# Warm-up dummies tied to one bank, one weight block loaded earlier, half-wise turning back and a classical second pair, with a new plan of the whole order, in an attention and feed-forward kernel

## The chip, the cores and the metric

The kernel runs on one core of a Trainium2 chip. The metric is device time in microseconds (us), from several runs of the same program; lower is better. Beside the times there is one profiled execution, whose trace lists every instruction of each engine: TensorE (PE for matmuls, PEld for its weight loads), VectorE (DVE), ScalarE (ACT), GpSimd (POOL) and SyncE (SP), and every transfer (DMA).

## What is computed

Attention over 4 batches, 8 heads, 768 tokens and head size 64, in which a token sees the 4 first tokens ("sinks") and the 128 last ones up to itself; then a feed-forward part over all 3072 tokens of 512 values, with 2048 hidden values and a squared relu:

```python
def _attn_ref(q, k, v, n_sink, window):
    scores = scale * np.matmul(q, k.transpose(0, 1, 3, 2))
    keep = is_sink | in_window          # pos < 4, or 0 <= rel < 128
    scores = np.where(keep, scores, -1000000000.0)
    a = np.exp(scores - np.max(scores, axis=-1, keepdims=True))
    return np.matmul(a / (np.sum(a, axis=-1, keepdims=True) + 1e-09), v)

def _moe_ref(x, w_in, w_out):
    r = np.maximum(x @ w_in, 0.0)
    return (r * r) @ w_out
```

Inputs and output are float32; the kernel's matmuls take bfloat16.

## The kernel before

**Work of a batch.** A batch has 6 token tiles of 128 tokens, taken as three pairs: tokens 0 to 255 (pair 0), 256 to 511 (pair 1), 512 to 767 (pair 2). q and k are brought into head-by-token form (`qkT`): in batches 0 and 1 by TensorE transposes into a PSUM tile `pt` (line 642) with a copy out of it (line 336 or 334), in batches 2 and 3 by transposing transfers that SP issues (line 596). For tokens 0 to 511 of batch 0, q and k come as float32 (`qr`, line 491) and are first cast to bfloat16 (`qs`); everything else is cast while it is loaded, by transfers from POOL's queue (`qn`, `v`, `w_in_sb`, `w_out_sb`). Then come the scores (`ps`, line 749; in pair 0 of batch 0 with a bias matmul, line 742), exp on ACT (`expm`, line 769), the window's mask (line 781 on DVE, or two selects on POOL, line 360), the scores of the sinks (`pk`, line 708), the values (`po`, line 817), a division by the sum (lines 833, 834), and the turning back of tokens into columns (`bridge`, `px`, line 866, copied to `xT`; in batches 2 and 3 a transposing transfer, line 848). Heads go in pairs; `m` is one of four such pairs.

**Feed-forward.** `layer1` (line 883) makes a block of 1024 hidden results a token tile's width at a time into a PSUM tile `pm` (line 894), 16 matmuls of 256 columns or 8 of 512; relu (line 905 on ACT, 907 on DVE) frees the bank, and a square (lines 914, 916) makes `gT`. There are four loads of `w_in`, each for four of the sixteen hidden blocks. The second product is taken for a pair of token tiles. `layer2` (line 920) is the classical form: 32 matmuls of 512 columns (line 935) in eight parts, and one copy out for each tile. `layer2_fast` (line 980) is a Strassen-Winograd form: four sums on DVE (line 1004), seven products of 8 matmuls of 256 columns (line 1046, named c, d, a, b, c, d, a), and sums of quarters on DVE and ACT (lines 1055 to 1116). It also needs four differences of `w_out`, made once on DVE (`weight_sums`, line 963). In batch 0, pair 0 is classical (line 1187) and all other pairs are fast.

**PSUM.** Two pools of two tiles, `att` and `den`, each tile two banks. `layer1` and the second product use `den`; attention uses `att`, and in batches 0 and 1 partly both.

**What sets the order.** The order on each engine isn't written out. `Plan.run` (line 185) is a list scheduler that runs while the kernel is built: each operation has a key (a due time), estimated costs by engine, its predecessors and the PSUM or SBUF slots that it takes. `PLACES` and `NUDGES` (lines 22 and 54) are tables of numbers that shift and stretch keys by group and by operation; `LATENCY` (line 17) and the transfer estimates (lines 19, 20, 471) enter the starts. So a change of any of these can move every instruction. Only the transfers are chained by hand, in the order in which lines 1133 to 1153 call the loads.

**Dummies.** `warm(dst)` (line 324) puts matmuls of the identity ahead of a block while the plan's time is below 34 us, as many as half of the planned gap holds at 0.056 us, at most 40. They write into the first half of the tile that the block will use, or into its half `h`. `touch` (line 341) declares which accesses to a tile lie in different banks, so that they don't wait for each other; dummies aren't told to it.

**The loads from POOL's queue** at the start: v of tokens 0 to 255, v of tokens 256 to 511, the four `w_in` blocks, q and k of tiles 4 and 5, v of these, the four `w_out` blocks, then batch 1.

**The turning back** (lines 858 to 880) is made in two halves of heads, each with its own copy; both wait for all norms (divisions) of the pair of tiles.

Of the kernel before, what the change touches and what calls it, by code (L numbers as in the profile page):

```python
# [12 lines left out]
BF16 = mybir.dt.bfloat16  # L13
# [3 lines left out]
LATENCY = 0.186  # L17
# [5 lines left out]
    ('att', 0, 0): (0.21, 1.17, -0.18), ('att', 0, 1): (-0.08, 1.08, 0.04), ('att', 0, 2): (0.015, 1.83, -0.6),  # L23
    ('att', 1, 0): (-0.085, 1.44, -0.04), ('att', 1, 1): (-3.34, 2.24, -0.4), ('att', 2, 0): (0.295, 1.46, 0),
    ('att', 2, 1): (-0.735, 0.82, -0.14), ('att', 2, 2): (0.025, 0.88, -0.04), ('att', 3, 0): (0.825, 0.51, 0.08),
    ('att', 3, 1): (0.095, 1.16, -0.02), ('att', 3, 2): (0.325, 0.67, 0.48), ('ev', 0, 1): (0.215, 0.47, 0.16),
    ('ev', 0, 2): (1.935, 1.29, -0), ('ev', 1, 0): (-0.22, 1.16, 0.06), ('ev', 1, 1): (-0.285, 0.65, 0.86),
    ('ev', 1, 2): (0.14, 0.86, -0.46), ('ev', 2, 0): (1.38, 1.32, 0.66), ('ev', 2, 1): (-0.32, 0.82, -0.4),
    ('ev', 2, 2): (0.3, 1.21, 0.76), ('ev', 3, 1): (-0.895, 0.85, -0.64), ('ev', 3, 2): (-0.26, 1, -0.38),
    ('l1', 0, 0): (-0.02, 0.85, 0), ('l1', 0, 1): (0.405, 1, 0.24), ('l1', 0, 2): (0, 0.79, -0.02),  # L30
    ('l1', 1, 0): (0.3, 1.96, 0.08), ('l1', 1, 2): (3.445, 0.3, 0.28), ('l1', 2, 0): (-0.385, 0.71, -0.22),
    ('l1', 2, 2): (-1.92, 1.74, 0.24), ('l1', 3, 0): (0.42, 1.87, 1.06), ('l1', 3, 2): (-0.165, 0.51, 0.16),
    ('l2', 0, 0): (0, 0.95, 0.08), ('l2', 0, 1): (0.22, 1.1, -0.04), ('l2', 0, 2): (-1, 1.11, 0.42),
    ('l2', 1, 0): (2.155, 0.65, 0.4), ('l2', 1, 1): (0.61, 0.79, -0.26), ('l2', 1, 2): (0.4, 1.99, -0.22),
    ('l2', 2, 0): (0.875, 0.26, -2.14), ('l2', 2, 1): (-0.115, 0.6, -0.08), ('l2', 2, 2): (-0.295, 0.98, -0.44),
    ('l2', 3, 0): (-0.02, 1.05, 0.2), ('l2', 3, 2): (-0.69, 0.96, 0.5), ('prep', 0, 0): (0.005, 1.06, -0.62),
    ('prep', 0, 1): (0.635, 0.51, -0.2), ('prep', 1, 0): (0.015, 1, 0), ('prep', 1, 1): (0.055, 1.01, -0.02),
    ('prep', 2, 0): (0.195, 1.11, 0.1), ('prep', 3, 0): (0, 0.84, 0), ('sink', 0, 0): (0.105, 0.86, -0.2),
    ('sink', 0, 1): (-0.105, 0.96, 0), ('sink', 1, 0): (0.93, 1.41, 0.22), ('sink', 1, 1): (-0.025, 1.08, -0.76),
    ('sink', 2, 0): (0.025, 0.99, -0.24), ('sink', 3, 0): (0.215, 1, 0), ('sum', 0, 1): (0, 1.16, -0.08),  # L40
    ('sum', 1, 0): (0.18, 0.44, -2.08), ('sum', 1, 1): (-2.945, 1.06, 1.12), ('sum', 1, 2): (-0.45, 2.49, -1.34),
    ('sum', 2, 0): (0.665, 0.25, 0.82), ('sum', 2, 1): (0, 2.44, 1.56), ('sum', 2, 2): (-0.28, 1.76, 0.08),
    ('sum', 3, 0): (-0.17, 1.59, 0.46), ('sum', 3, 1): (-0.725, 0.7, -0.46), ('sum', 3, 2): (0.055, 0.7, 0.36),
    ('turn', 0, 0): (-0.175, 0.89, 0.1), ('turn', 0, 1): (0.18, 0.58, -0.68), ('turn', 0, 2): (-0.03, 1.45, -0.2),
    ('turn', 1, 0): (-0.195, 1.03, 0.18), ('turn', 1, 1): (-0.035, 0.63, 0.46),
    ('turn', 1, 2): (-0.585, 1.98, -2.12), ('turn', 2, 0): (0.015, 0.99, 0.38),
    ('turn', 2, 1): (-0.365, 1.36, -0.38), ('turn', 2, 2): (0, 0.98, 0.32), ('turn', 3, 0): (-0.1, 1.14, -0.28),
    ('turn', 3, 1): (-0.16, 1.26, -0.72), ('turn', 3, 2): (0.025, 0.92, -0.1), ('val', 0, 0): (-1.295, 0.62, -0.4),
    ('val', 0, 1): (0, 0.95, 0.16), ('val', 0, 2): (0.155, 1.03, -0.5), ('val', 1, 0): (0.015, 0.93, 0),
    ('val', 1, 1): (-0.145, 0.98, 0), ('val', 1, 2): (0.04, 1.25, 0.08), ('val', 2, 0): (-1.09, 0.51, -1.08),  # L50
    ('val', 2, 1): (-0.015, 0.93, -0.28), ('val', 2, 2): (-0.235, 0.96, -0.24), ('val', 3, 0): (-0.245, 0.84, 0.08),
    ('val', 3, 1): (0.755, 2.5, -0.58), ('val', 3, 2): (1.78, 2.4, 0.76), ('wt', 0): (-0.14, 1.32, -0.32),
}
NUDGES = {
    4: (-0.25, 0.48), 16: (-0.103, -0.3), 17: (0.038, -0.06), 18: (0.083, 0.08), 19: (0.017, -0.28),
    20: (0.005, -0.12), 21: (-0.026, -0.38), 23: (-0.015, 0.38), 24: (0.111, 0.4), 25: (-0.017, -0.2),
    26: (0.014, -2.46), 27: (0.063, -0.74), 28: (-0.07, -0.12), 29: (-0.064, 0.02), 30: (-0.047, -0.76),
    31: (-0.001, -0.04), 32: (0.102, 1.86), 33: (0.261, 0.22), 34: (-0.211, -0.62), 35: (0.056, 0.08),
    36: (0.061, -0.32), 37: (-0.006, 0.32), 38: (-0.013, -0.16), 40: (-0.269, -1.14), 41: (0, 0.04),
    42: (0.024, 0.16), 43: (-0.059, -0.22), 44: (0, -0.66), 45: (-0.003, 0), 46: (0.043, 0.26), 47: (0.059, -0.02),  # L60
    48: (0.013, 0.18), 49: (0.124, 0.08), 50: (0.004, -0.26), 51: (-0.136, 0.02), 52: (-0.049, 0.1),
    53: (-0.159, -1.08), 54: (0, 0.02), 56: (0.067, -0.6), 57: (0, 0.02), 60: (-0.263, 0.58), 61: (-0.153, -0.44),
    62: (-0.003, 0.66), 64: (-0.003, 0), 65: (0.037, 0), 66: (-0.097, 0), 67: (-0.046, 0.46), 68: (-0.002, -0.06),
    69: (0.035, 0.36), 70: (-0.001, -0), 72: (0.291, -0.52), 73: (0, -0.08), 74: (-0.036, 0.94), 75: (0.15, 0.32),
    76: (0.011, 0), 77: (0.008, 0.96), 78: (-0.024, 0.12), 80: (-0.015, 0.76), 81: (-0.139, 0.24), 82: (-0.002, 0),
    83: (0.01, 0.02), 84: (0.213, -0.06), 85: (0, -0.08), 86: (0.063, -0), 87: (-0.175, -0.2), 88: (0.107, 0.16),
    89: (0, 0.08), 90: (-0.001, 0.1), 91: (-0.657, 0.04), 93: (-0.008, 0.14), 94: (0.003, 0.1), 95: (0, -0.14),
    96: (-0.002, -0.34), 97: (0.019, -0.18), 98: (0.406, 0.84), 99: (0.027, 0.06), 100: (0.113, 1.1),
    101: (-0.031, 0), 102: (0.23, 0.96), 104: (0.103, 0), 105: (0.005, 0), 106: (-0.073, -0.4), 107: (0.108, -0.4),
    109: (-0.009, 0), 110: (0.403, 0.66), 111: (0.405, 0.56), 112: (0.003, -0.34), 113: (-0.056, 0.2),  # L70
    116: (-0.199, 0.7), 118: (0.001, 0.02), 119: (0.108, 0.72), 120: (0.101, 0.18), 121: (0, -0.22),
    122: (-0.22, -0.52), 124: (-0.004, 0.04), 125: (0.004, 0), 126: (0.03, 0.52), 127: (0.116, -0.3),
    129: (0.001, 0.1), 130: (0.006, -0.14), 131: (0.119, -0), 132: (-0.003, 0.04), 134: (-0.008, 0),
    135: (-0.352, 0.32), 136: (-0.299, 0.48), 138: (-0.093, -0.06), 139: (0.157, -0.2), 140: (0.067, 0.5),
    141: (0.005, 0), 142: (-0.106, -0.4), 143: (-0.12, 0.46), 144: (0.004, 0), 145: (-0.15, -0.48),
    146: (-0.007, -0.26), 147: (0, 0.2), 148: (0, -0.14), 149: (0.177, 0.66), 150: (-0.355, -1.88),
    151: (0.001, 0.14), 152: (-0.098, 0), 153: (-0.035, 1.38), 155: (0.012, 0), 156: (0, 0.08),
    157: (-0.089, -0.02), 159: (0.057, -1), 160: (0.168, -1.88), 161: (-0.004, -0.18), 162: (0.047, -0.08),
    163: (0, -0.6), 164: (-0.073, 0.08), 165: (-0.032, 0), 166: (-0.004, 0), 167: (-0.302, -0.06),
    168: (0.377, 0.62), 169: (0, -0.14), 170: (-0.277, -0.92), 171: (-0.012, -0.38), 172: (0.119, 0.86),  # L80
    173: (0.031, 0.56), 174: (-0.06, -0.52), 176: (0, -0.38), 177: (0.051, -0.42), 178: (-0.009, 0),
    180: (-0.375, -0.08), 181: (-0.432, 1.04), 183: (0.386, -0.12), 184: (-0.014, 1.16), 185: (-0.027, -0.08),
    186: (-0.114, 0), 188: (0.093, -0.74), 189: (0.391, 0.06), 191: (-0.01, -1.12), 192: (0.023, 0),
    193: (0.001, -0.58), 194: (0.116, 0.16), 195: (0.016, 0.04), 197: (0.278, -0.1), 198: (-0.228, 0.08),
    199: (-0.593, -0.7), 200: (-0.017, 0), 201: (-0.016, -0.18), 202: (-0.011, 0.16), 205: (0.016, -0.06),
    206: (-0.312, -0.04), 207: (0, -1.04), 208: (0.018, -0.02), 209: (0.069, -0.26), 210: (0.405, -0.24),
    211: (0.007, -0.36), 212: (0.148, 0), 213: (0.195, 0.2), 214: (-0.14, -1.18), 215: (-0.006, 0),
    216: (0.058, -0.6), 217: (0.015, 0.06), 218: (0.121, 0.56), 219: (0.009, -0.28), 220: (-0.112, 0.08),
    221: (0.051, 0.44), 222: (0.078, 0.16), 224: (0, -0.02), 225: (-0.16, -0.96), 226: (-0.589, -1.1),
# [172 lines left out]
def kernel(  # L262
# [11 lines left out]
    nc = tc.nc  # L274
# [954 lines left out]
```

## Time and profile before

| what | us |
|---|---|
| median of 3 runs | 219.59 (219.2 to 219.82) |
| the profiled execution, its own time | 219.53 |
| its span, first to last instruction | 217.5 |
| TensorE matmuls busy | 206.9 (95% of the span) |
| DVE busy | 150.1 (69%) |
| ACT busy | 117.8 (54%) |
| POOL busy | 97.3 (45%) |
| granted TensorE clock, mean | 0.999 |

The profile has several views. The page gives busy time and the span in 40 slices, one digit for tenths of a slice. The view by stage gives the busy time of each engine between two moments. The chain in order of time follows the work that ended last back to what released it; each of its pieces has a start, a length and what it was. The timeline lists instructions in order of time, with a count, and in square brackets how long the engine sat idle before and what released it. A line number such as L894 is that of the kernel before. All times are counted from the first instruction.

### The profile page before, as it was taken

To read this page: it belongs to the slowest core of one execution; us is meant where nothing else is said; L and a number is where in the kernel's file an instruction comes from. 1 tells how busy PE (TensorE), PEld (TensorE's weight loads), DVE (VectorE), ACT (ScalarE), POOL (GpSimd) and SP (SyncE) were. 2 spreads that over 40 slices of the span, in tenths; PEclk is the share of its full clock that TensorE was granted. 3 is DMA by queue.
4 is the path that set the end of the run, shared out by engine and by line. 5 is a ranking of instruction groups with operands and counts; after the bars stand their busy time and mean duration, and the time that the engine had idled before them with its cause. 6 is when DMAs were issued, how large, how long until landed. Compare 5 with 4: busy or idle time off the path is not lost.

```text
span 217.5 us, 5286 instructions
## 1 busy us (share of the span) xinstructions
PE 206.9 (95%) x2222; PEld 163.5 (75%) x2225; DVE 150.1 (69%) x280; ACT 117.8 (54%) x149; POOL 97.3 (45%) x134
## 2 busy tenths in 40 slices
PE   7799899999999999996999999999999999999992
PEld 7558795689878855585988775579887775799892
DVE  5565476698898837599687755667886747476942
ACT  2596557466765668878570744576512353663210
POOL 7997877699998383589453000410340000000000
PEclk9999999999999999999999999999999999999999
DMA  5999999999999999999979962001303113002022
GB/s 188 264 179 205 165 210 205 158 112 203 155 131 149 196 164 174 132 129 126 106 92 151 190 167 103 0 0 27 65 10 142 53 24 121 3 2 96 3 96 96
DMA packets 93351, 26.06 MB, mean 120 GB/s; under 512 B 86800, under 2 KB 91280, under 8 KB 93328
## 3 DMA queue, kind: packets, MB, share of 16 engines
q0 software_dynamic: 69248, 12.59, 79.1%
q1 hardware_dynamic: 23896, 13.07, 27.9%
q8 instruction: 17, 0.28, 0.5%
q10 hardware_dynamic: 184, 0.07, 0.1%
q14 instruction: 6, 0.05, 0.1%
HBM read 27.30 MB, written 6.29 MB: 154 GB/s over the span
## 4 chain that ended last, share of the span: by engine, by line
PE 81%; POOL 5%; DMA 5%; DVE 4%; ACT 2%; issue 1%; POOLq 0%
PE pm L894 33%; PE py L1046 31%; PE po L817 6%; PE ps L749 4%; DMA w_in_sb<-in_moe_w_in_dram 4%; PE py L935 3%; POOL v L521 2%; DVE sg L1004 2%; PE pt L642 2%; DMA qr<-in_k_dram 1%; POOL expm L360 1%; DVE r L907 1%; PE px L866 1%; ACT expm L769 1%; PE ya L1046 1%; POOL vs L690 1%
## 5 line engine op out<-in xcount | busy, mean ns | idle before, releaser
L894 PE MATMUL pm<-xT,w_in_sb 128*128 128x256 bf16 (+1 forms) x576 | 89.2, 308 | 1.8 <-DVE r L907 1.6
L894 PEld LDWEIGHTS <-w_in_sb 128*128 128x128 bf16 x576 | 62.3, 114 | 20.9 <-issue 3.3
L905 ACT ACTIVATE r<-pm 128x1024 bf16<-128x1024 f32 x39 | 40.0, 1025 | 42.4 <-PE pm L894 39.9
L769 ACT ACTIVATE expm<-ps 128x1024 bf16<-128x1024 f32 (+1 forms) x48 | 43.4, 953 | 20.3 <-PE ps L749 20.2
L360 POOL TENSOR_SCALAR_AFFINE_SELECT expm<-expm 128x512 bf16<-128x512 bf16 x34 | 24.8, 756 | 49.9 <-ACT expm L769 47.3
L1046 PEld LDWEIGHTS <-gT 128*128 128x128 bf16 x368 | 34.1, 98 | 4.6 <-issue 0.6
L916 DVE TENSOR_TENSOR gT<-r 128x1024 bf16<-128x1024 bf16 x34 | 24.3, 716 | 16.0 <-ACT r L905 15.6
L1046 PEld LDWEIGHTS <-sg 128*128 128x128 bf16 x264 | 25.0, 98 | 3.8 <-issue 0.3
L1046 PE MATMUL py<-wt,gT 128*128 128x256 bf16 x176 | 22.8, 273 | 0.0
L1046 PE MATMUL py<-wt,sg 128*128 128x256 bf16 x176 | 22.5, 273 | 0.0
L1046 PE MATMUL py<-w_out_sb,gT 128*128 128x256 bf16 x160 | 20.8, 273 | 0.0
L817 PEld LDWEIGHTS <-expm 128*128 128x128 bf16 x352 | 16.6, 97 | 3.7 <-POOL expm L360 1.2
L817 PE MATMUL po<-v,expm 128*128 128x65 bf16 x352 | 18.3, 193 | 1.1 <-POOL expm L360 0.9
L834 DVE TENSOR_TENSOR xn_sb<-po,rc 128x512 bf16<-128x512 f32 (+1 forms) x28 | 17.2, 615 | 1.0
L914 ACT ACTIVATE gT<-r 128x1024 bf16<-128x1024 bf16 x14 | 14.6, 1055 | 0.3
L749 PE MATMUL ps<-qkT 64*128 64x128 bf16 (+1 forms) x256 | 14.6, 238 | 0.0
L781 DVE TENSOR_TENSOR expm<-expm,tri 128x1024 bf16<-128x1024 bf16 x15 | 10.8, 723 | 4.8 <-ACT expm L769 3.1
L749 PEld LDWEIGHTS <-qkT 64*128 64x128 bf16 x256 | 8.0, 94 | 7.5 <-issue 6.4
L833 DVE RECIPROCAL rc<-po 128x8 f32<-128x8 f32 (+1 forms) x28 | 5.5, 197 | 11.7 <-PE po L817 11.6
L817 PE MATMUL po<-vs,es 128*128 128x65 bf16 x128 | 13.0, 193 | 0.0
L907 DVE TENSOR_SCALAR r<-pm 128x1024 bf16<-128x1024 f32 x9 | 11.0, 1220 | 2.3 <-PE pm L894 2.3
L817 PEld LDWEIGHTS <-es 128*128 128x128 bf16 x128 | 11.7, 97 | 0.0
(77 smaller groups left out, 250.9 us busy)
## 6 DMA issues: line engine op xcount, KB each, us to landing
out_dram<-osb SPq DMA_DIRECT2D x11, 512.0 KB, 2.8
v<-in_v_dram POOLq DMA_DIRECT2D x24, 128.0 KB, 5.6
qn<-in_k_dram POOLq DMA_DIRECT2D x20, 128.0 KB, 9.5
qn<-in_q_dram POOLq DMA_DIRECT2D x20, 128.0 KB, 8.0
w_in_sb<-in_moe_w_in_dram POOLq DMA_DIRECT2D x4, 512.0 KB, 10.4
w_out_sb<-in_moe_w_out_dram POOLq DMA_DIRECT2D x4, 512.0 KB, 10.6
qr<-in_k_dram SPq DMA_DIRECT2D x4, 256.0 KB, 5.2
qr<-in_q_dram SPq DMA_DIRECT2D x4, 256.0 KB, 5.0
```

The lines of the kernel that those rows point to most:

```text
L360: nc.gpsimd.affine_select(out=e_tile, in_=e_tile, compare_op=ALU.is_ge, fill=fill, base=i - 1, pattern=[[0, n], [1 if i else -1, 128]], ch ...
L749: nc.tensor.matmul(ps[:, h2, o:o + w], lhsT=qkT_sb[r, m, 1, c, :], rhs=qkT_sb[r, m, 0, qb:qb + w // 128, :], start=(i == 0 and not biased) ...
L769: nc.scalar.activation(out=x[:, :, o:512], in_=bank_t["s", b, s, m][:, :, o:512], func=AF.Exp, scale=scale)
L781: nc.vector.tensor_mul(y, y, tri.rearrange("p (o a) c -> p o (a c)", o=1).to_broadcast([128, 4, 256]))
L817: touch(("po", b, s, m0), e, nc.tensor.matmul(pv[:, i, h2, :], lhsT=lhsT, rhs=rhs, start=(n_ == 0), stop=(n_ == len(mms) - 1)), j)
L834: touch(("po", b, s, m0), e, nc.vector.tensor_tensor(out=xn_sb[:, 2 * s:2 * s + 2, 128 * (m0 + j0):128 * (m0 + j0 + nj)].rearrange("p i (j ...
L894: nc.tensor.matmul(pm[:, i, :], lhsT=w_in_sb[:, fb // 4, kb, fb % 4:512:4], rhs=xT[:, c0 // 256:(c0 + cw) // 256, kb, :], start=(kb == 0), ...
L905: nc.scalar.activation(out=o, in_=h, func=AF.Relu)
L907: nc.vector.tensor_scalar_max(o, h, 0.0)
L914: nc.scalar.activation(out=g, in_=r, func=AF.Square)
L916: nc.vector.tensor_mul(g, r, r)
L1046: ins = nc.tensor.matmul(y_, lhsT=x[:, i, :], rhs=r_, start=(first or tail and n == 2) and i == 0, stop=i == HB - 1, skip_group_check=not ...
```

## The change

- `warm` takes the name of the tile and its half, tells `touch` of each dummy, and makes at most 26 of them instead of 40.
- `w_in` block 0 is loaded behind v of tokens 0 to 255 and ahead of v of tokens 256 to 511.
- Each half of the turning back waits for the norms of its own heads.
- In batch 0, pair 1 is classical too.
- The plan's numbers are new: `LATENCY`, one transfer estimate, one surcharge on a load, and the two tables `PLACES` and `NUDGES` in full. No operation has other arithmetic by this.

```diff
-LATENCY = 0.186
+LATENCY = 0.122
...
-    def warm(dst):
+    def warm(dst, key=None, h=0):
...
         if P.now < WARM_UNTIL:
-            for _ in range(min(40, int(0.5 * P.gap / 0.056))):
-                nc.tensor.matmul(dst, lhsT=ident, rhs=ident, start=True, stop=True,
-                                 is_transpose=dst.dtype == BF16)
+            for _ in range(min(26, int(0.5 * P.gap / 0.056))):
+                ins = nc.tensor.matmul(dst, lhsT=ident, rhs=ident, start=True, stop=True,
+                                       is_transpose=dst.dtype == BF16)
+                if key:
+                    touch(key, "pe", ins, h)
...
-    ROW = {512: 0.03, 1024: 0.046}
+    ROW = {512: 0.03, 1024: 0.052}
...
-(0.7 if (b, m0, ti, g) == (0, 1, 1, 0) else 0.0)
+(0.7 if (b, m0, ti, g) == (0, 0, 0, 0) else 0.0)
...
-                        warm(pt[:, 0, 0:128])
+                        warm(pt[:, 0, 0:128], ("pt", b, m, g))
...
-                            warm(po[:, js[0], 0:128])
+                            warm(po[:, js[0], 0:128], ("po", b, s, m0), js[0])
...
-                        warm(px[:, h, 0:128])
+                        warm(px[:, h, 0:128], ("px", b, s), h)
...
-                    br = op(at(fs + 0.36), {"pe": 0.235}, bridge, after=norms + older_layer1,
+                    br = op(at(fs + 0.36), {"pe": 0.235}, bridge,
+                            after=norms[len(norms) * h // 2:len(norms) * (h + 1) // 2] + older_layer1,
...
     load_v(0, 0, None, [("qk", 0, 3, 0, 0)])
+    load_w_in(0)
     load_v(0, 1)
-    for i in range(4):
-        load_w_in(i, None if i == 0 else None)
+    for i in range(1, 4):
+        load_w_in(i)
...
-            if b == 0 and u < 1:
+            if b == 0 and u < 2:
                 layer2(b, u, lambda i, part, u=u: 0.408 + 0.466 * (4 * part + 2 * u + i) / 24, by_part=True)
```

What the scheduler makes of it, as the built program shows: the first burst has 26 dummies instead of 39, then four transposes, then ten more dummies. POOL's queue begins with two v tiles, `w_in` block 0, the third v tile, a cast of a k tile, the fourth v tile, `w_in` blocks 1 and 2, the triangles, two selects, the masks, and `w_in` block 3; before, it had four v tiles, four `w_in` blocks, four q and k tiles, a v tile, the triangles, the masks and four selects. On TensorE, the third `w_in` block's matmuls come right behind the turning back of pair 1. The first part of batch 0's classical pair 1 comes just ahead of the transposes of batch 1's last two token tiles, the other seven between there and the first layer-1 block of batch 1; the fast pair 2 now comes within that stretch too. In batch 1 the layer-1 blocks of tokens 512 to 767 now come ahead of those of tokens 0 to 511, whose eight relus all stand on ACT. SP's store of pair 1 stands ahead of the last six of batch 2's twelve transposing transfers, behind the store of pair 2.

## Prediction

> **What bounds the kernel now.** First the page's header and slices, then busy time by stage, then the chain in order of time, then the timeline of the first 25 us.
>
> ```profile
> span 217.5 us, 5286 instructions
> ...
> PE   7799899999999999996999999999999999999992
> ```
>
> TensorE is idle only in slices 0 to 1, a little in 2 to 4, in one slice near 100 us, and in the last. I cut the stages there:
>
> ```profile
> 0.00:24.40 24.40, 19.67 (x269) 16.03 (x270) 13.78 (x39) 15.33 (x20) 21.19 (x38) 1.00 1.29 206
> 24.40:56.49 32.09, 31.92 (x347) 26.43 (x347) 24.24 (x42) 19.95 (x25) 26.47 (x34) 1.00 1.81 174
> 56.49:100.40 43.91, 43.91 (x502) 32.13 (x499) 33.61 (x62) 30.73 (x40) 30.88 (x41) 1.00 2.18 154
> 100.40:102.40 2.00, 0.36 (x6) 0.17 (x6) 2.00 (x3) 1.93 (x2) 1.99 (x4) 1.00 1.27 86
> 102.40:213.50 111.10, 111.09 (x1112) 88.70 (x1111) 76.40 (x137) 49.59 (x63) 16.73 (x22) 1.00 0.40 72
> ```
>
> Columns: length, then busy time of PE, PEld, DVE, ACT, POOL. From 24.4 to 213.5 us TensorE runs back to back but for 2 us, while DVE is full in exactly those 2 us. So there are three things to win: the start, the pause at 100, and TensorE work itself. The chain shows what made the first two:
>
> ```profile
> 9.69 7.63 DMA w_in_sb<-in_moe_w_in_dram
> ...
> 17.61 0.88 POOL v L521
> ...
> 18.55 0.56 POOL tri L360 x2
> ...
> 21.14 2.51 POOL expm L360 x4
> ...
> 23.69 0.87 PE po L817 x23
> ...
> 98.89 2.30 DVE sg L1004
> 101.19 1.15 DVE r L907
> ...
> 102.38 1.91 PE pm L894 x16
> ```
>
> At the start POOL waits for a w_in landing before it can issue a v load, and only then builds triangles and masks for which TensorE stands until 23.7. At 100 us the layer-1 block waits for its bank, held by a relu queued on DVE behind four Winograd sums. And the dummies:
>
> ```profile
> 1.50 4.17 PE L329 MATMUL pt<-ident 128*128 128x128 bf16 x39 [1.50 <-POOL ident L384]
> ...
> 6.58 0.38 PE L329 MATMUL pt<-ident 128*128 128x128 bf16 x4 [0.69 <-ACT qkT L334]
> ...
> 10.07 0.38 PE L329 MATMUL pt<-ident 128*128 128x128 bf16 x4 [0.89 <-ACT qkT L334]
> ...
> 15.06 0.27 PE L329 MATMUL po<-ident 128*128 128x128 bf16 x2 [0.41 <-DVE xn_sb L834]
> ```
>
> A dummy waits for the reader of the tile's other half, and the true transposes or values stand behind it.
>
> **Part by part.** *Dummies.* The cap goes from 40 to 26. The first burst is 39 x 107 ns = 4.2 us and ends at 5.5; 26 end at 1.50 + 2.8 = 4.3, while the first cast is ready at 4.1 (3.65 + 0.43): 1.2 us earlier for the first transpose. The waits of 0.69, 0.89 and 0.41 go, since a dummy is now tied to its own bank. What is late next is the load: the last q tile is cast at 10.37, so the later half of the front moves by about 0.6 us at most from this. Against the smaller cap speaks the Trainium skill ("TensorE: Matmul & The Clock Gate", "What's actually happening"): full clock comes only after about 3.4 us of sustained work, and 26 dummies are 2.8. The trace went to 56 ns spacing 3.85 us after its first dummy. By the rule alone, with 26 dummies and then idleness, one more window at half speed doubles about 1 us of real matmuls: +1 us in the front. But four transposes and ten more dummies now follow at once (14 x 107 ns = 1.5), so work is unbroken to about 5.7: I take 0, range 0 to +1, and even +1 lies in slack shown below.
>
> *First weight block earlier.* On POOL's queue its issue (0.77) moves past two v issues (0.88 to 1.1 each). Loads land one after another: v at about one per us from 11.3 to 14.2, then w_in at 17.3 (9.69 + 7.6) and 19.9 (10.44 + 9.4), the last at 25.0. So block 0 lands at about 12.3 + 3 = 15.3, the two passed v tiles at about 17.3 instead of 14.2, and blocks 1 to 3 where they were. The values of tokens 256 to 511 first run at 19.43 now, behind a layer-1 block; in the new order they come at about 18.5, so the v delay is covered by 1 us (without cover: up to 1).
>
> *Turning back in halves.* The first half needs only two norms instead of four. DVE's two copies (0.42 each) then no longer both follow the last norm: about 0.3 us, no instructions added.
>
> *POOL.* In the new order triangles (0.56) and one select stand ahead of w_in block 3, masks too; v tiles 4 and 5 no longer stand ahead of the triangles. POOL takes one cast of a k tile (nearest row: its 128x512 copy, 0.61), ahead of the fourth v issue. Block 3 is then issued at about 18 instead of 11.9, still 4 us ahead of block 2's landing (22.5), so the load stream isn't starved; cost 0, up to +1.
>
> With these, layer 1 starts at about 16.7 instead of 17.68, its second block at 19.9 (its weights), the third at 22.5 (its weights land 11.17 + 11.3) instead of 24.40: the front gains 1.9 us.
>
> *Where that goes.* From there to the transposes of batch 1's last two token tiles the new order has ten layer-1 blocks at 1.75, nine classical parts at 0.87 and about 7.0 us of transposes, scores, sinks and values: 32.3 us, so TensorE arrives at 54.8. (Before, 24.40 to 56.49 held 32.1: one part less, one turning back of 0.45 more, 0.2 of small gaps.) But the last q tile is issued at 49.96 and lands 6.1 us later, at 56.03; the load engines were busy without a break until then, and the bytes ahead of it are the same. So these transposes start at about 56.1 instead of 56.49. Of the 1.9 us, 0.2 pay for more work ahead, 1.3 become a new wait for a load, 0.4 are kept. Behind that wait stand, on TensorE, the second score block of tokens 256 to 511 of batch 1 and the next classical part, and behind them ACT's exps and DVE's sums for the third pair; they have nothing else to do, so the wait costs its own length and no more.
>
> *Classical second pair.* 32 matmuls of 512 columns at 0.215 (four in 0.86 in the chain) = 6.9 against 56 of 256 at 0.109 (eight in 0.87) = 6.1: +0.8 us of TensorE, in full, as it is the bound. 0.87 of it stands ahead of 56.1, where TensorE would wait anyway, so behind that point the work is 0.06 less than before. DVE loses four sums (0.69 each) and about 2 us of quarter sums for one eviction near 0.6. On SP the pair's store now stands ahead of the q transposes of batch 2's tiles 2 and 3: it waits for the eviction near 76.1, where the old store let them go at 77.4 (landing 86.5); scores need them at 88.6 by the same walk. Covered by 2 us.
>
> *The pause at 100.* The fourth sum took 2.38 us where the first took 0.69: it began at 98.81, while POOL issued a load to 99.19 and then ran two selects to 100.43. The skill ("SBUF — State Buffer", "Who interferes with whom") has a DVE operation with two SBUF inputs blocked for the whole of a GpSimd instruction that reads SBUF, by which whoever starts first goes first: the sum would have been done at 99.5. The row shows it behind the load issue too; by the row each such sum is a risk of 1.7 us. In the new order, the layer-1 blocks of batch 1's first 512 tokens come behind those of the last 256, all their relus stand on ACT, and no sums of that pair lie between them. I walked the queues: relus of 1.02 against block pairs of 1.73, plus eight exps; each bank comes free 0.5 to 2 us ahead of use. So I take the pause (2.03) as gone.
>
> *Sum.* Behind 56.49 the old run has 157.0 us to its last matmul; less 2.03 and 0.1 of small waits, less 0.06: 154.8. 56.1 + 154.8 = 210.9, plus the unchanged tail of 4.0 (213.5 to 217.5): span 214.9. The profiled execution took 219.53 for 217.5, 2.03 around it: 216.9. It stands 0.06 below the median of 219.59, which I neglect.
>
> **Rivals.** (1) *The pause comes back*, as ACT or DVE become the bound around 85 to 105 or in the stretch where the classical pair and the next fast pair both hold a "den" bank (55 to 68) and attention has two "att" banks left. For it: ACT has some 15.5 us of relus and exps in 16.5 us there. Against it: the slack above. 1 to 2 us return: 217.9 to 218.9, likeliest 218.5. Chance 0.28.
> (2) *The load isn't the limit* at 56: were q ready by 54.8, all the front's gain is kept, 1.2 less: 215.6. For it: POOL issues the last loads late, and may issue them 0.6 earlier; against: the unbroken load share of slices 1 to 20. Chance 0.12.
> (3) *Slower.* The classical pair holds its bank for 20 us (54.8 to 75.5, in pieces between other work). In that time seven score blocks and transposes need both "att" banks, each freed only after two exps (1.94 a pair) of the block before; the slack I found for three of them is 0.5 us. If ACT slips past it, each block waits for its exps: 7 x 0.6 = 4.2 on top: 221.1. It decides from 2.7 us of such waits on. Nothing in the old run shows it, as there no pair shared the banks for so long. Chance 0.05.
> (4) *The new order changes nothing*: front gain all lost at the load, pause replaced in full: 219.6. Chance 0.03.
> The forecast has 0.52.
>
> **Numbers.** A measurement can tell 0.3% (0.66 us) from no change. Faster than 218.9: forecast 0.52, (2) 0.12, three quarters of (1), 0.21: 0.85. Within: 0.09; slower 0.06. The range reaches from (2) to the upper end of (1): 215.5 to 218.9; the forecast alone with its unknowns (clock 0 to +1, waits of 0 to 0.8) is 216.2 to 217.7.
>
> **What would show it.** Dummies of the first burst end near 4.3 and no dummy waits for ACT or DVE. First layer-1 block near 16.7, third near 22.5. A PE wait of about 1 us released by a qn load near 55 to 56. No gap over 0.5 us from 57 to the end, PE's last matmul near 210.9. I am wrong if the first clock row is later than 6.5, if PE waits for exps or norms between 57 and 75, or for a relu between 85 and 105.

## The result, and the profile after

The changed kernel takes 217.34 us (median; 216.81 to 217.92) against 219.63 for the kernel before in the same comparison: ratio 0.990, 95% interval 0.987 to 0.993, 2.2 us faster. The prediction was 216.9. The changed kernel's profiled execution took 216.81 us, the least of its four, for a span of 215.1. A few executions of some kernels took over 1.5% more than the fastest of the same kernel; they are left out of all ratios and counts below.

The page's header and TensorE slices after the change:

```profile
span 215.1 us, 5182 instructions
...
PE   7999989999999999999999999999999999999992
```

The pit near 100 us (a 6 before) is gone; a small one is left in slice 5, that is at 27 to 32 us. The stages, cut where they answer to those of before (third layer-1 block, the wait in slice 5, the transposes of batch 1's last tokens, the last matmul); columns as there: length, then busy time of PE, PEld, DVE, ACT, POOL:

```profile
0.00:21.94 21.94, 19.92 (x261) 16.08 (x261) 15.52 (x44) 14.33 (x19) 19.44 (x37) 1.00 1.19 206
21.94:27.30 5.36, 5.36 (x50) 5.35 (x50) 1.91 (x6) 4.02 (x5) 1.98 (x4) 1.00 2.12 167
27.30:28.62 1.32, 0.42 (x5) 0.12 (x4) 0.00 (x0) 0.00 (x0) 0.91 (x2) 1.00 2.07 183
28.62:55.48 26.86, 26.65 (x286) 21.03 (x290) 19.86 (x32) 17.75 (x21) 19.70 (x27) 1.00 1.83 184
55.48:211.20 155.72, 155.10 (x1582) 118.43 (x1583) 107.78 (x196) 81.40 (x103) 46.91 (x60) 1.00 0.92 96
```

Length minus the first busy column is TensorE's idle time. The third block comes at 21.94 instead of 24.40 (2.46 gained); the middle takes 33.54 instead of 32.09 (1.45 lost: 0.9 idle at 27.3 to 28.6, 0.5 more work, the rest small gaps); the end takes 155.72 instead of 157.0 (1.3 gained, of which 1.0 is idle time, 1.65 before and 0.62 now). Sum: 2.3. This is one execution, with an early front. In a second profile of the same instructions (after_again, below) the third block comes at 23.10, and in four other runs with this order of the front (q_ahead, more_dummies, no_dummies, combined) at 23.00 to 23.40; in relu_ahead and sum_last, which have the old front, at 24.96 and 24.18. So the front usually gains some 1.3 us, and the middle loses less.

The chain of waits in order of time, and TensorE's timeline, show what the front now hangs on. In the timeline the brackets hold the idle time ahead of a row and what ended it:

```profile
7.89 7.74 DMA w_in_sb<-in_moe_w_in_dram
...
15.88 2.61 POOL qn L507 x3
18.50 10.07 DMA qn<-in_q_dram
...
28.61 0.45 PE pt L637 x5
```

```profile
1.50 2.96 PE L322 MATMUL pt<-ident 128*128 128x128 bf16 x26 [1.50 <-POOL ident L379]
4.25 0.63 PE L637 MATMUL pt<-ident,qs 128*128 128x128 bf16 x4
4.68 1.38 PE L322 MATMUL pt<-ident 128*128 128x128 bf16 x11
...
16.25 1.93 PE L890 MATMUL pm<-xT,w_in_sb 128*128 128x256 bf16 x16
...
28.61 0.45 PE L637 MATMUL pt<-ident,qn 128*128 128x128 bf16 x5 [0.73 <-DMA qn<-in_q_dram]
```

GpSimd's selects and triangles, on the chain before, are off it; the q tiles of batch 0's last 256 tokens are on it. TensorE asks for them at 27.2, 2.9 us earlier than before (30.09), and they land no earlier. The row of before, then loads from the program's view of these tiles, of before and of after (the last line is the time from issue to landing):

```profile
30.09 1.06 PE L642 MATMUL pt<-ident,qn 128*128 128x128 bf16 x16
```

```profile
L512 POOL DMA_DIRECT2D qn<-in_q_dram x2: 950/954/958, 14.4 to 15.2; - x2
...
DMA to landing us min/median/max: 13.3/13.4/13.4
```

```profile
L507 POOL DMA_DIRECT2D qn<-in_q_dram x2: 903/907/911, 17.6 to 18.5; - x2
...
DMA to landing us min/median/max: 9.9/10.0/10.1
```

Issued 3.2 us later, they land at the same time: 15.2 + 13.4 = 28.6 before, 18.5 + 10.1 = 28.6 after. The bytes ahead of them set it, not the issue: where a 512 KB block is taken from ahead of them (q_ahead, below), they are issued at 17.0 and 17.9 and land at 25.0 and 25.8.

### The profile page after: what moved, and what is told of

It reads as the page before. It is cut to its first block, busy times and chain, and to the rows that moved or that the text cites. A ratio compares the mean times of both kernels' runs of the same rounds, so it can differ in the third digit from the quotient of the medians.

```text
span 215.1 us, 5182 instructions
## 1 busy us (share of the span) xinstructions
PE 207.5 (96%) x2177; PEld 161.0 (75%) x2184; DVE 145.1 (67%) x276; ACT 117.8 (55%) x147; POOL 88.9 (41%) x127
## 4 chain that ended last, share of the span: by engine, by line
PE 81%; DMA 8%; DVE 4%; POOL 3%; issue 1%; ACT 1%; POOLq 0%
PE pm L890 35%; PE py L1042 28%; PE po L812 6%; PE py L931 6%; DMA qn<-in_q_dram 5%; PE ps L744 4%; DMA w_in_sb<-in_moe_w_in_dram 4%; POOL qn L507 1%; PE pt L637 1%; POOL v L516 1%; DVE qkT L331 1%; PE ya L1042 1%; POOL vs L685 1%; PE px L861 1%; DVE r L903 1%
## 5 line engine op out<-in xcount | busy, mean ns | idle before, releaser
L901 ACT ACTIVATE r<-pm 128x1024 bf16<-128x1024 f32 x41 | 42.0, 1025 | 38.9 <-PE pm L890 37.4
L355 POOL TENSOR_SCALAR_AFFINE_SELECT expm<-expm 128x512 bf16<-128x512 bf16 x26 | 18.2, 725 | 44.6 <-ACT expm L764 37.2
L1042 PEld LDWEIGHTS <-gT 128*128 128x128 bf16 x336 | 31.3, 98 | 3.7 <-issue 0.3
L1042 PEld LDWEIGHTS <-sg 128*128 128x128 bf16 x240 | 22.8, 98 | 3.9 <-issue 0.9
L1042 PE MATMUL py<-wt,gT 128*128 128x256 bf16 x160 | 20.7, 273 | 0.0
L1042 PE MATMUL py<-w_out_sb,gT 128*128 128x256 bf16 x144 | 18.7, 273 | 0.0
L829 DVE TENSOR_TENSOR xn_sb<-po,rc 128x512 bf16<-128x512 f32 (+1 forms) x28 | 17.2, 615 | 1.0
L812 PE MATMUL po<-v,expm 128*128 128x65 bf16 x352 | 17.3, 193 | 0.3 <-DMA v<-in_v_dram 0.3
L776 DVE TENSOR_TENSOR expm<-expm,tri 128x1024 bf16<-128x1024 bf16 x19 | 13.4, 711 | 4.8 <-ACT expm L764 4.8
L931 PE MATMUL py<-w_out_sb,gT 128*128 128x512 bf16 x57 | 14.6, 380 | 0.5 <-issue 0.2
L329 ACT ACTIVATE osb<-py 128x256 f32<-128x256 f32 (+1 forms) x13 | 5.6, 434 | 13.2 <-PE py L1042 7.7
L545 POOL DMA_DIRECT2D v<-in_v_dram x12 | 10.6, 901 | 4.0 <-PE po L812 4.0
```

Source lines behind the costliest of these rows:

```text
L355: nc.gpsimd.affine_select(out=e_tile, in_=e_tile, compare_op=ALU.is_ge, fill=fill, base=i - 1, pattern=[[0, n], [1 if i else -1, 128]], ch ...
L776: nc.vector.tensor_mul(y, y, tri.rearrange("p (o a) c -> p o (a c)", o=1).to_broadcast([128, 4, 256]))
L812: touch(("po", b, s, m0), e, nc.tensor.matmul(pv[:, i, h2, :], lhsT=lhsT, rhs=rhs, start=(n_ == 0), stop=(n_ == len(mms) - 1)), j)
L829: touch(("po", b, s, m0), e, nc.vector.tensor_tensor(out=xn_sb[:, 2 * s:2 * s + 2, 128 * (m0 + j0):128 * (m0 + j0 + nj)].rearrange("p i (j ...
L901: nc.scalar.activation(out=o, in_=h, func=AF.Relu)
L931: touch((b, u), e, nc.tensor.matmul(pm[:, i, :], lhsT=gT_sb[t // 4][:, fb, 128 * (t % 4):128 * (t % 4) + 128], rhs=w_out_sb[:, fb, :], sta ...
```

## The experiments

**Theory.** The change is worth two things, about 1 us of front (the rest of the front's gain is taken by the next load that is late) and about 1.3 us of the pause at 100. **Rivals.** One part alone carries it: the load order, the dummies (by their waits or by the clock), or the repair of the pause.

The plan orders the whole program anew for any edit. So each experiment replays the order that a plan had chosen (instructions, engines and banks), written out as a list, and a diff shows the rows of that list that move. Changes in us are (ratio minus 1) times 219.6.

**The front in the old order.** First the load alone:

```diff
 GpSimd: v tile 0, v tile 1
+w_in block 0
 v tile 2, v tile 3
-w_in block 0
 w_in blocks 1, 2, 3
```

> The kernel before with the whole order of its work kept, only the first w_in block's load is issued ahead of the v loads of tokens 256 to 511. Theory A (the prediction's: the load order lifts the front): first layer-1 block near 16.7 instead of 17.68, third one 0.7 to 1.2 us ahead of 24.40, end 0.5 to 1.2 earlier: 218.4 to 219.1. Theory B (GpSimd's queue sets the third block: triangles, masks and selects still stand behind a v issue that waits for a w_in landing): first block earlier as in A, third within 0.3 of 24.40, end 219.3 to 219.7.

Measured: ratio 1.0019 (1.0002 to 1.0036), 0.4 us slower. TensorE's timeline, behind the first layer-1 block:

```profile
20.33 0.24 PE L817 MATMUL po<-v,expm 128*128 128x65 bf16 x2 [0.95 <-DVE expm L781]
...
24.08 0.20 PE L817 MATMUL po<-v,expm 128*128 128x65 bf16 x1 [0.38 <-POOL expm L360]
```

The first block comes earlier (17.37), but the values behind it then wait for masks and selects, and the third block stands at 24.79. So it is theory B in kind (slower than its 219.3 to 219.7): the load order alone lifts nothing. Then all of the front's moves together, still in the old order behind them:

```diff
 v tile 0, v tile 1
+w_in block 0
 v tile 2, v tile 3
-w_in block 0
 w_in blocks 1, 2
+triangles, masks
 w_in block 3, k and q tiles 4 and 5, v tile 4
-triangles, masks
```

and the change's edits of the dummies.

> The kernel before with the order of its work kept behind the front; in the front all three moves of the change: dummies capped at 26 and tied to their own bank, first w_in block ahead of the v loads of tokens 256 to 511, triangles and masks built ahead of the fourth w_in block's issue. Third layer-1 block near 22.4 instead of 24.40 by all theories. Theory A (loads take the front's gain back, as the prediction said, at the last q tile of batch 1, which lands at 56.0 in this order): TensorE waits 0.4 for the q tiles of batch 0 near 28.2 and 1 for batch 1's last one near 55; 0.5 us is kept: 219.1 (218.9 to 219.3). Theory C (only the q tiles of batch 0, landing near 28.6, take something): 1.4 kept: 218.2. Theory D (no load takes it): 1.9 kept: 217.7.

Measured: ratio 0.9960 (0.9945 to 0.9975), 0.9 us faster. The third block comes at 22.82. TensorE's waits between 40 and 60 us (total, times, longest):

```profile
PE pt L644 <- DMA qn<-in_q_dram: 1.4, 2, 0.7
```

These are batch 1's q tiles, at 48.9 and 57.1. So A in kind: of 1.6 us won at the third block, loads take a part back. In size it lies between A and C. The profiled execution took 220.0, the most of the 16, and ends no earlier than the kernel before; the median (218.57) keeps about 1 us, so in most executions the loads take less than this profile shows. Whether it is the store that makes these tiles late:

```diff
 SyncE:
-store of the first pair
 DMA transpose of batch 2's first k tile
+store of the first pair
```

> The kernel front_all (the order of before with all of the front's moves), but the store of the first output pair, 512 KB issued at 47 to 49 us among the loads for batch 1, is queued on SyncE behind the first DMA transpose near 59. Theory A (the store's bytes lie ahead of batch 1's last q tile, and that is why the front's gain is lost in the old order): that tile lands near 54.5 to 55 instead of 57.1, the wait of 0.86 at 56 goes, and the end is 0.7 to 1.0 earlier than front_all (timed 218.57): 217.6 to 217.9. Theory G (the tile is late for the order of the loads, not for the store): it lands after 56.5, within 0.3 of front_all. Theory H (the store collides with the loads of batch 2 instead): the wait at 56 goes and comes back at batch 2's transposes or scores: 218.3 to 218.8.

Measured: ratio 0.9964 (0.9953 to 0.9975), the same as front_all. The last q tile does land at 54.8 instead of 57.1 and nothing waits at 56, as A said. But the time didn't follow. In its profiled execution another load was late:

```profile
26.19 0.52 PE L896 MATMUL pm<-xT,w_in_sb 128*128 128x256 bf16 x3 [0.80 <-DMA w_in_sb<-in_moe_w_in_dram]
```

The fourth w_in block landed at 26.1 here, 24.8 in front_all. That is ahead of the place where the two kernels differ, so it is a difference between two executions. Such a difference also stands in the 2.3 us (57.1 less 54.8). The q tile that landed last before the store was issued came at 46.9 in front_all and at 45.7 in late_store, so some 1.3 of the 2.3 was there already, and at most 1.0 is the store's. From batch 1's earlier q tile to its last one it takes 7.5 us in late_store (47.3 to 54.8), 8.3 in front_all (48.8 to 57.1) and 9.3 in the kernel before (46.8 to 56.1): a store among the loads delays the tile behind it by 0.8 to 1.8 us. That this costs time is not shown; why the medians are equal stays open.

**The wait at 28 in the new order.**

```diff
 GpSimd: triangles, select, masks
-w_in block 3
 k and q tiles 4 and 5 of batch 0
+w_in block 3
 TensorE, layer-1 blocks (token range, feature blocks):
-(0, 12 to 15), transposes, (256, 12 to 15), (256, 8 to 11), (256, 4 to 7)
+(256, 8 to 11), transposes, (256, 4 to 7), (0, 12 to 15), (256, 12 to 15)
```

The relus and squares of these blocks move with them, one relu from VectorE to ScalarE and one the other way.

> The changed kernel with the whole order of its work kept, but the fourth w_in block is loaded behind the k and q tiles of tokens 512 to 767 of batch 0 instead of ahead of them, and the two layer-1 blocks that need it change places with the two that don't. Theory A (the wait of 1 us at 27.3 to 28.6 is one for bytes in the load stream): these q tiles land near 26.0 instead of 28.56, the wait goes, the fourth w_in block lands near 28.6 and is first used at 30.5; end 1.0 earlier, at 216.3 (216.1 to 216.6). Theory B (a later load takes it back, the q tile landing at 47.3 or the one at 53.9): the wait goes and comes back there: 217.0 to 217.4. Theory E (the tiles are late because GpSimd issues them late, 18.5 us): they are issued only 0.8 us earlier and land near 27.8: 216.6 to 216.9.

Measured: ratio 0.9885 (0.986 to 0.991), 217.07. The q tiles land at 25.8 and nothing waits for them; E falls. In the profiled execution the third block came only at 23.00, so that the transposes began at 28.23 and would have waited for some 0.4. Between A and B the time can't decide: it is 0.3 us below the changed kernel, inside both intervals, though the wait that B sends to a later load is not seen before 60 us. How much the front moves from one execution to the next, the changed kernel's second profile tells (same instructions, order replayed):

> The changed kernel once more, its plan's order written out as a list instead of being worked out (the same instructions on each engine), timed together with the three others. All theories: 217.3 us (216.9 to 217.7); its trace shows how far the front alone varies from one execution to the next (first layer-1 block at 16.25 in the one and 17.51 in the last kernel, whose front is the same).

Measured: ratio 0.9906 (0.988 to 0.993), 217.24. Its stages:

```profile
0.00:23.10 23.10, 18.48 (x261) 14.68 (x261) 17.09 (x44) 14.22 (x19) 19.70 (x38) 1.00 1.22 204
23.10:55.82 32.72, 32.24 (x340) 26.43 (x342) 21.94 (x38) 21.86 (x26) 22.34 (x31) 1.00 1.87 178
55.82:211.54 155.72, 155.09 (x1582) 118.42 (x1583) 107.79 (x196) 81.49 (x103) 46.89 (x60) 1.00 0.89 96
```

This is the clearest test of the theory: one program, two executions, the third block 1.16 us apart (21.94 and 23.10), the end 0.34 apart (211.20 and 211.54). The early one waits 0.9 for the q tiles, the late one 0.3 (total, times, longest, from 24 to 60 us; the early one first):

```profile
PE pt L637 <- DMA qn<-in_q_dram: 0.9, 2, 0.7
```

```profile
PE pt L637 <- DMA qn<-in_q_dram: 0.3, 1, 0.3
```

The stretch behind is 155.72 in both. And the load order undone in the new order:

```diff
-w_in block 0
 v tile 2, v tile 3
+w_in block 0
```

> The changed kernel with its order kept, but the first w_in block is loaded behind the v tiles of tokens 256 to 511 again. It lands near 17.4 instead of 15.6, the first layer-1 block starts near 17.6, the third near 23.1 to 23.3 instead of 21.94. Theory A (the q tiles set the pace from 28.6 on): TensorE is at the transposes of batch 0's last tokens at 28.4 to 28.6, its wait of 1 us there is gone, and the end moves by 0 to 0.3 us. Theory F (the load order carries a part of the gain): 1.0 to 1.4 us slower than the changed kernel.

Measured: ratio 0.9937 (0.992 to 0.995), 0.7 us slower than the changed kernel, between A and F. In the profile the first w_in block lands at 16.8, the first layer-1 block waits for it, and the end is at 211.33, between the changed kernel's two (211.20 and 211.54): the profile speaks for A. The median has more in it. In 4 of its 20 executions the mean clock was 0.989 to 0.992, and these took 218.2 to 219.4 us; the experiments on the dummies show such a loss of clock. The other 16 have a median of 217.7, still some 0.4 above the changed kernel (217.24 and 217.34 in its two timings). Whether that is the load order is not settled.

**The pause at 100.**

```diff
 VectorE: three sums
-fourth sum
 relu that frees the bank
+fourth sum
 two masks
```

> The kernel before with the whole order of its work kept (each instruction, engine and bank as its plan chose them), but the one relu that frees the bank near 101 us stands ahead of the fourth Winograd sum on VectorE instead of behind it. Theory A (the pause at 100 is nothing but this queue): the relu runs at about 98.9 to 100.1, TensorE's next layer-1 block starts right behind the sink scores at 100.73 instead of 102.38, and nothing later takes the 1.65 us back: 218.0 us (217.8 to 218.2). Theory B (VectorE is full there, so the pause only moves: the delayed sum or the masks behind it make TensorE wait at the next products or values): 219.2 to 219.6.

Measured: ratio 0.9977 (0.996 to 0.999), 0.5 us faster. VectorE's timeline, and TensorE's waits from 90 to 110 us:

```profile
99.60 1.21 DVE L907 TENSOR_SCALAR r<-pm 128x1024 bf16<-128x1024 f32 x1
100.74 1.24 DVE L1004 TENSOR_TENSOR sg<-gT,sg 128x1024 bf16<-128x1024 bf16 x1
101.90 2.13 DVE L778 TENSOR_TENSOR expm<-expm,mask 128x768 bf16<-128x768 bf16 x2
```

```profile
PE po L817 <- DVE expm L778: 0.7, 1, 0.7
```

The bank comes free in time, and the next values wait for the masks, which the sum now delays: theory B in kind, with slightly more gain than it allowed. With the sum behind the masks too:

```diff
 VectorE: three sums
-fourth sum
 relu that frees the bank, two masks
+fourth sum
```

> The kernel before with its order kept, but the fourth Winograd sum stands behind both the relu and the two masks that it held up on VectorE, ready for the product that needs it near 104.5. In relu_ahead the relu alone gave 0.5 us, as the masks then came late. Theory A (the pause is this one sum's place in the queue, and its whole 1.65 us can be had): no wait at the layer-1 block (100.73) and none at the values; 1.4 to 1.7 us less than before, ratio 0.9923 to 0.9936. Theory B (VectorE has no room there, and whatever stands last holds the next product): 0.3 to 0.9 us less, ratio 0.996 to 0.9985.

Measured: ratio 0.9940 (0.992 to 0.996), 1.3 us faster, a little under A's 1.4 to 1.7, which the interval covers. From batch 1's last transposes (56.36) to the last matmul, TensorE is idle for 0.01 us:

```profile
56.36:211.68 155.32, 155.31 (x1614) 120.88 (x1611) 111.91 (x200) 82.25 (x104) 49.93 (x64) 1.00 0.93 97
```

Theory A: moving one sum in a queue takes the pause away, if it goes behind both instructions whose readers wait, and not behind one. By the profile it is worth 157.0 - 155.3 = 1.7. Another repair was not tried. In the kernel before, this sum was not only early but long:

```profile
98.81 2.38 DVE L1004 TENSOR_TENSOR sg<-gT,sg 128x1024 bf16<-128x1024 bf16 x1
```

The median of its kind is 0.69. The excess of 1.7 us is as long as the pause, and GpSimd was busy beside it with a load issue and two selects (98.29 to 100.43). In sum_last VectorE's two masks stand beside the selects and take 2.38 instead of 1.14, and TensorE waits for neither. So moving GpSimd's selects might have done as much as moving the sum; no run shows it.

**The dummies.** Not tied to their own bank (the cap stays at 26):

```diff
-warm(pt[:, 0, 0:128], ("pt", b, m, g))
+warm(pt[:, 0, 0:128])
```

and in the same way for the "po" and "px" tiles.

> The changed kernel with its order kept, but the dummies are not tied to their own bank, so that each waits for the reader of the tile's other half again. Theory A (the q tiles that land near 28.6 set the pace from there on, so that up to 1 us of front is worth nothing): waits of 0.3 to 0.8 us in front of dummies come back before 10 us, the third layer-1 block moves by less than that, the wait at 28 shrinks by as much: within 0.3 us of the changed kernel. Theory F (the dummies' bank carries a part of the gain): 0.5 to 0.9 us slower than the changed kernel.

Measured: ratio 0.9957 (0.993 to 0.998), 1.1 us slower than the changed kernel: F, and more than it said. The profiled execution (220.22) is one of those left out and is read for the order of events only. By stretches (the column behind POOL's is the granted clock):

```profile
13.75:17.17 3.42, 1.27 (x23) 0.79 (x22) 3.27 (x8) 1.69 (x3) 3.36 (x8) 1.00 1.84 184
17.17:20.58 3.41, 3.34 (x36) 2.32 (x36) 1.71 (x6) 2.05 (x3) 3.41 (x5) 0.50 1.24 206
20.58:23.99 3.41, 3.41 (x67) 3.39 (x66) 2.37 (x6) 2.45 (x3) 2.03 (x3) 1.00 1.48 194
```

In the first stretch a dummy waits 1.5 us for VectorE's norm, TensorE is busy for 1.27 of 3.42, and for the next 3.41 the clock is at half. Half the clock for 3.41 us of 219 is a mean of 0.992, and ten of this kernel's 20 executions have that mean, at 219.1 to 219.7 us (median 219.4); the other ten, with 0.998 or more, lie at 216.6 to 218.4 (median 217.55, 0.2 to 0.3 above the changed kernel). So the waits cost little by themselves; most of the loss is the clock that goes with them.

The risk comes with the new order. None of the 130 executions of the kernel before that were timed beside these runs has a mean clock below 0.995, and none of the 38 of front_all and late_store, which have the change's dummies in the old order. Of the 16 in the new order with tied dummies (the changed kernel, after_again, q_ahead), three have 0.990 to 0.992. More dummies, and none:

```diff
-            for _ in range(min(26, int(0.5 * P.gap / 0.056))):
+            for _ in range(min(26, int(1.0 * P.gap / 0.056))):
```

> The changed kernel with its order kept and nearly twice the dummies outside the first burst (a whole planned gap filled instead of half of it). Theory K (what the dummies are worth is the granted clock: it falls to half for 3.4 us after a stretch in which TensorE was busy for some 0.4 of the time, which costs 1.7 us in a part of the runs): no run below a mean clock of 0.995, against 3 of 16 of the kernels with the changed front, median 0.1 to 0.4 us better than 217.3, ratio 0.988 to 0.990. Theory L (more of them only stand in front of true work): same clocks, 0.2 to 1 us slower than the changed kernel, ratio 0.991 to 0.994.

Measured: ratio 0.9892 (0.987 to 0.992), 217.08; no execution below 0.998. That is what K said of the clocks, but six executions are too few to show it: at 3 in 16, six without a loss come about in three cases of ten. The time can't be told from the changed kernel's.

```diff
-            for _ in range(min(26, int(0.5 * P.gap / 0.056))):
+            for _ in range(min(0, int(0.5 * P.gap / 0.056))):
```

> The changed kernel with its order kept and no dummies at all. Theory K (they are worth the clock): full clock comes 3 us later or is lost again for 3.4 us near 14 to 17, the true matmuls of the front take twice their time there, and 1 us of it at most is hidden by the wait for the q tiles at 28: 218.5 to 220.5, ratio 0.996 to 1.005, most runs with a mean clock of 0.992 or less. Theory L (the front is paced by loads and VectorE, the clock matters little): within 0.4 us of the changed kernel, ratio 0.989 to 0.9925.

Measured: ratio 0.9898 (0.988 to 0.992), 217.56, as the changed kernel: K falls, and L holds. So in the new order the tied dummies bring no gain that these runs can show. The clock does come late, as four score matmuls show before and after 13.5 us (the view by stage gives 1.00 here too, since it has no record ahead of the first row of full clock, so the slow start is read from durations):

```profile
12.52 0.50 PE L744 MATMUL ps<-qkT 64*128 64x256 bf16 x4
...
13.84 0.34 PE L744 MATMUL ps<-qkT 64*128 64x256 bf16 x4
```

But all that runs at half speed until then has slack: the third block starts at 23.30, where the changed kernel has 21.94 and 23.10, and the q tiles land at 28.6 in any case. From 13.48 on TensorE is busy and the clock stays.

**All together.** q_ahead, more_dummies, and

```diff
 VectorE:
-two copies of batch 1's sink keys
 copy of q, three sums for the third pair
+two copies of batch 1's sink keys
```

> The changed kernel with three things together: the fourth w_in block behind the q tiles of tokens 512 to 767 as in q_ahead, the dummies of more_dummies, and VectorE's first sums for the third output pair ahead of the two copies of batch 1's sink keys, which are not needed before 67 us. The last takes away the wait of 0.23 at 57.4. Theory M (small waits of TensorE add up, as nothing else is near): no wait at 28 nor at 57.4, 0.3 to 0.8 us better than the changed kernel, ratio 0.9865 to 0.9885. Theory N (behind 28 TensorE stands on VectorE's and ScalarE's queues anyway, and the wait at 28 is short in most executions): within 0.3 us of the changed kernel, ratio 0.989 to 0.991.

Measured: 216.17 us, ratio 0.9843 (0.983 to 0.986), 3.4 us faster than before and 1.2 to 1.4 better than the changed kernel (0.9906 and 0.9899). The profiled execution shows no wait at 28 and none at 57.4, but it took 216.76, above its median, and the two waits are worth 0.5 to 1.1 by the profiles above. It goes beyond M, and what the excess is made of is not shown.

What was not tried: the classical second pair and the halves alone, since both change the list itself; triangles and masks ahead without the load order or the dummies, so what front_all owes to each is open; front_all and sum_last together, so that the two parts add is taken from their sum alone.

## Where the prediction was right and where not

The time, 216.9 for 217.34, is well inside the range, and the two places of the gain were named rightly: front_all (0.9, 0.55 to 1.2) and sum_last (1.3, 0.8 to 1.8) add to 2.2, and so does the change. But that the total is so close is in part luck. Of its two large terms, the front's was too small (0.4 us kept at the last transposes of batch 1; 1.0 and 0.7 in the two profiles), and the end's too large (2.2 us; 1.3 in both). Point by point:

- **The front's start.** Predicted 16.7, 19.9 and 22.5 for three layer-1 blocks; 16.25, 19.51 and 21.94 in one profile, 17.61, 20.85 and 23.10 in the other, and the later one is the usual one. The landings were right (first w_in block 15.6 for 15.3, the passed v tiles 16.6 and 17.5 for 17.3). The gain was read from the loads, with GpSimd's new order at cost 0; but the load order without the triangles and masks ahead lifts nothing (w_in_first), so that order is part of the gain. Its row at 19.43 for the values of tokens 256 to 511 holds two dummies; the values begin at 19.88, which changes nothing.
- **"1.3 become a new wait for a load"** at batch 1's last transposes, since the tile lands at 56.03. This step failed in its place. The tile landed at 54.0, and TensorE asked for it only at 55.48. In the new order the store is issued at 50.4, behind the tile (49.0), and not at 48.8, ahead of it; "the bytes ahead of it are the same" overlooked the store, worth up to 1.8 us by late_store. But the front met another load first: batch 0's q tiles at 28.6, which in the old order had 1.4 us to spare (30.09 against 28.67). The walk compared one load with TensorE's arrival, not each load on its way. 0.9 us went there in one profile and 0.3 in the other, and the transposes began at 55.48 and 55.82 instead of 56.1.
- **The pause.** "So I take the pause (2.03) as gone": it is. The term was oversized twice. Its idle time was 1.65 (the 2.03 held the sink scores' own time), and 0.62 us of small waits stand behind 55.48 where I put none, for a relu before 78.1 (0.2), a copy before 85.3, a sum before 57.7, and some 0.3 ahead of parts of the classical pair, for which the profile names no releaser. They are rival 1 in small. So the end took 155.7, not 154.8. This 0.9 and the 0.6 from the step before nearly cancel, which is luck. The reading that a load issue held the long sum ("the row shows it behind the load issue too") stays open: in relu_ahead the same sum, started during the selects, ended at 101.98, inside a load issue (101.16 to 102.05).
- **Classical pair.** Predicted 0.2 more work ahead of the transposes and 0.06 less behind; TensorE's busy time rose by 0.5 ahead and fell by 0.3 behind, and the waits of 0.3 just named take that back. No run separates it from the rest of the plan.
- **Dummies.** The first true transpose at 4.25 (predicted 4.3), no dummy waits for ACT or VectorE, both right. "I am wrong if the first clock row is later than 6.5": this row, the first record of full clock, came at 7.17 in the first profile and at 4.18 in the second, whose end is 0.34 later; without dummies it comes at 13.48, and the time is still the same. The sign was no sign. That a late clock is covered by the front's slack was right; that the clock can be lost again later, where nothing covers it, was missed.
- **GpSimd's order.** Block 3 was issued at 15.1, not 18, cost 0 as predicted; the q tiles, 3 us later in the queue, cost 0 as well.
- **Halves.** As intended, the first half starts at 15.25, ahead of the end of the fourth norm (15.14 to 15.57), and the second right behind it. No run separates the 0.3 us of this step.
- **Rivals.** (2) said right that the load at 56 is no limit and wrong that all is then kept. (3) didn't happen: no wait for exps while the pair held its bank.

## What to carry to other kernels

When a front is made faster, list every load that TensorE meets after it with its landing time and the time it is asked for: the smallest difference is all that is kept until that load is moved. When an instruction early in a queue holds up what others wait for, move it behind all of these: here behind one it gave 0.5 us, behind both 1.3. And ask why it was long. Judge an edit at the start of a kernel by several executions, as its start may differ by over 1 us from one to the next while the end differs by 0.3.

## What was not expected of the hardware

- The granted clock fell after one stretch of 3.42 us with TensorE 37% busy (1.27 us), though no single wait in it was over 1.5 us; a stretch with 59% (2.02 of 3.41, from 7.60 to 11.01 in after_again) kept it. It stayed at half for 3.41 us. On the way up, stretches with 66% (2.25 of 3.41, 0.34 to 3.75 in the changed kernel's profile) and 68% (2.31, 3.24 to 6.65 in no_dummies) did not raise it, and one with 79% (2.68, 0.77 to 4.18 in after_again) did. These stretches are counted in steps of 3.41 us from the moments at which the clock changed; in loose_dummies the rise at 6.93 and the fall at 17.17 lie three such steps apart. That stretches are fixed windows of this length agrees with the Trainium skill ("TensorE: Matmul & The Clock Gate", "What's actually happening").
- Waiting dummies were worse than none: 0.9957 tied to nothing, 0.9898 without any. In loose_dummies' profile they raise the clock at 6.9 us, and it is lost again at 17.2, just ahead of the layer-1 blocks; without them it comes at 13.5 and stays.
- A load issued 3.2 us later in a full stream landed within 0.1 us of the same time (28.7 and 28.6).
